# Layer 1 of an attention and two-layer MoE kernel: column tiles in pairs with banks of their own, subtractions of GpSimd tied to VectorE, wider weight pieces

## Chip, core and metric

The kernel runs on one core of one Trainium2 chip. The metric is the device time of one execution in microseconds (us). PE is TensorE, DVE is VectorE, ACT is ScalarE, POOL is GpSimd, SP is SyncE, which issues the transfers.

## What is computed

Sigmoid attention feeds a first layer with g = h cos(h), which feeds a second layer with a rational function. 4 batches of 448 tokens, 12 heads of 64 (model width 768), hidden width 2048 in both layers:

```python
attn = 1.0 / (1.0 + np.exp(-(scale * q @ k.T - np.log(S))))
x = attn @ v                                  # (1792, 768)
h = x @ w1_in;  y = (h * np.cos(h)) @ w1_out  # layer 1
h = y @ w2_in                                 # layer 2
P = a[0] + a[1]*h + a[2]*h**2 + a[3]*h**3
Q = 1.0 + abs(b[0])*abs(h) + abs(b[1])*h**2
out = (P / (Q + 1e-06)) @ w2_out
```

The four weight matrices are given as float64.

## The kernel before, in words

**Numbers.** Every operand of a product is held as a scaled pair of fp16 values (high and low part), and a product is three matmuls (high by high, high by low, low by high). No engine reads float64: a piece of weights is loaded as pairs of 32-bit words (`f64_load`, line 111), `f64_value` (line 119) puts f32 values together in three DVE passes (one tensor_scalar, two scalar_tensor_tensor, all recorded at the helpers' lines 80 and 83), a scale by row or by row of tiles comes from the largest value or from the sum of the magnitudes, and a split writes high part (ACT) and low part (DVE).

**Layer 1, per batch bt.** The 2048 hidden columns are 16 tiles f of 128. One tile is 18 matmuls of 128x448 into one PSUM bank (`h_matmul`, line 564, matmul at line 570), from a pool of four banks (`PS`, line 73; the pools stand at lines 593 and 594). A chain of operations then makes g = h cos(h): `kk` on ACT (line 854) rounds h/(2 pi) to int32 in `k`; `r0` on DVE subtracts it (`r<-hx,ck,k`); `sn` on ACT (line 861) takes the sine; `r1` on DVE multiplies by h again out of the bank (`r<-hx,kap,r`) and by that frees the bank; `gh` on ACT (line 868) writes the high half of g, `gl` on GpSimd (line 871) the low half by a subtraction. The output of layer 1 is six column blocks e of 128, each a sum over all 16 f: 48 matmuls into one bank of the same pool (`o1_unit`, line 888, matmul at line 901). For batch 0 all six e are open at once (e = 4 and 5 in one of the two-bank tiles `xv`, `yw`, made by `wide`, line 600), with f outermost; for batches 1 and 2 they come as (0,1), 2, 3, 4, 5. Batch 3's are laid between the matmuls of layer 2. All of h of a batch stands before all of its o.

**What else DVE does meanwhile.** In the stretch of layer 1 it converts w1_out (tiles `f1o`, `v1o`, `wo`; used by o of batch 0), w2_out (`f2o`, `v2o`), and w2_in, all in pieces 384 wide. w2_in is read twice: once for the largest value of a row (`w2i_max_nodes`, line 1000: a load and a TENSOR_REDUCE `m2i` for each of 36 pieces), and again for the values, which are added and subtracted among four quarters and split (`w2i_nodes`, line 1026). The split pairs go to scratch in DRAM and are streamed back in layer 2.

**What sets the order.** A planner writes one fixed order for all engines before anything runs. Each operation is a node (line 619) with an engine, an assumed duration (`C448`, `C896` and the like, lines 612 to 617), predecessors, and counted resources that it takes and gives back (`stock`, line 1542: "ps" the banks, "f64" the load slots, "g", "kr" and others). `arrange` (line 650) follows the PE order as written from line 1450 on, and for the other engines takes whichever ready node is due first. Each engine and the SP queue then run their list in order: an instruction that waits holds up those behind it on the same engine.

Of the kernel before, what the change touches and what calls it, by code (L numbers as in the profile page):

```python
# [23 lines left out]
def sigmoid_attention_moe_cos_moe_rational(  # L24
# [17 lines left out]
    P = 128  # L42
# [13 lines left out]
    up = ctx.enter_context(tc.tile_pool(name="up", bufs=34))  # L56
# [107 lines left out]
    EARLY = 0  # L164
# [49 lines left out]
    m1o, s1o, i1o = (col(n, NF) for n in ("m1o", "s1o", "i1o"))  # L214
# [12 lines left out]
    with tc.manual_schedule():  # L227
# [160 lines left out]
        def add_w1o(f):  # L388
            def fin():
                row_scale(m1o[:, f:f + 1], s1o[:, f:f + 1], i1o[:, f:f + 1], f"1o{f}")  # L390
                wo[f] = wo_tile(f, 1)

            key = ("o", f)
            cells.append(
                (
                    value_ops(st_w, key, w1_out, f, 0, DM, lambda: m1o[:, f:f + 1], f"1o_{f}"),
                    split_ops(st_w, key, lambda: wo[f], s1o[:, f:f + 1], 0, DM),
                )
            )
            after[len(cells) - 1] = ((0.6, fin), range(len(cells) - 1, len(cells)))  # L400

# [92 lines left out]
        rho, irho, kap1 = col("rho"), col("irho"), col("kap1", NF)  # L494
# [69 lines left out]
        def h_matmul(pfx, bt, f):  # L564
            ps = PS(f"h{pfx}_{bt}_{f}")
# [49 lines left out]
        class Node:  # L615

            def __init__(self, eng, dur, fn, deps=(), acq=None, rel=None, due=None, soon=False, rush=False):
                self.eng, self.dur, self.fn = eng, dur, fn
                self.deps = [d for d in deps if d is not None]
                self.acq, self.rel = acq or {}, rel or {}  # L620
                self.due, self.soon, self.rush, self.end = due, soon, rush, None
                self.users, self.weak, self.after = [], (), None
# [14 lines left out]
        def N(eng, dur, fn, deps=(), acq=None, rel=None, due=None, soon=False, rush=False):  # L637
            n = Node(eng, dur, fn, deps, acq, rel, due, soon, rush)
# [8 lines left out]
        def nop():  # L647
            pass

        def arrange(stock, groups, start):  # L650
# [53 lines left out]
            def fresh(n):  # L704
                ready[n] = max([d.end + lat(d, n) for d in n.deps], default=start)
# [29 lines left out]
            while len(queue) < total:  # L735
                best = None
                cand = []
                for n in floats:
                    t = when(n)
                    if t is not None and t <= now["PE"]:  # L740
# [28 lines left out]
                for e in ("A", "V", "G", "D"):  # L769
                    c = [(r, n) for n in avail[e] for r in (when(n),) if r is not None]  # L770
                    if not c:
# [3 lines left out]
                    b_ = (max(r, now[e]), 1, n, None)  # L775
# [8 lines left out]
                t, _, n, src = best  # L784
                if n.eng == "PE":
# [15 lines left out]
        def x_nodes():  # L801
# [6 lines left out]
            for bt in range(1, B):  # L808
                for d in range(ND):
# [16 lines left out]
        def h1_nodes(bt):  # L826
# [764 lines left out]
```

## Time and profile before

| | |
|---|---|
| Time, median of 3 runs (lowest, highest) | 1024.26 us (1024.0, 1024.3) |
| The profiled execution: its time, its span | 1022.71 us, 1020.9 us |
| Mean granted clock of TensorE in it | 0.993 |
| Instructions of DVE, ACT, POOL (whole program) | 1450, 923, 75 |
| Matmuls of h in layer 1, of o in layer 1 | 1152, 1152 |

The profile comes from one execution. Busy time counts the instructions of an engine; a window's row gives the busy time of each engine in a stretch of the span, and PEclk there is the clock that TensorE was granted, where 1.00 is the upper of its two levels, 2.4 GHz, and lower values mean that part of the stretch ran at 1.2 GHz. The waits name what ended the idle time before an instruction. The chain that ended last is followed back from the last instruction to what released each.

### The profile page before, as it was taken

The page shows a single profiled execution, that of the slowest core. Times are in us where ns is not written, and L with a number is a line of the kernel's source. Part 1 is how long each engine was busy: PE and PEld are TensorE (multiplying, and loading weights), DVE is VectorE, ACT ScalarE, POOL GpSimd, SP SyncE. Part 2 cuts the span into 40 slices and gives each one's busy share as a digit, 9 for nine tenths or more (in the row PEclk, how much of TensorE's full clock was granted, in tenths as well). Part 3 has the DMA queues.
Part 4 walks back from the last instruction along what each step waited for, and adds up shares of the span by engine and source line. Part 5 has one row for each costly group of instructions (what it writes and reads, how often), then busy time and mean ns, then how long its engine had stood idle before and what let it go on. Part 6 is the DMA issues. An engine that isn't in the chain of part 4 may idle for free.

```text
span 1020.9 us, 14605 instructions
## 1 busy us (share of the span) xinstructions
PE 994.9 (97%) x5399; PEld 501.6 (49%) x5399; DVE 805.6 (79%) x1450; ACT 600.7 (59%) x923; POOL 77.0 (8%) x75
## 2 busy tenths in 40 slices
PE   9999999889999999889999999999999999999998
PEld 4444445445555554445555455555554555555554
DVE  6999969999899899999993688889927898870000
ACT  7999967634676446644664577676506767750000
POOL 0000003310132002210032000000000000000000
PEclk9999999989999999999999999999999999999999
DMA  8788952457667885567102132133122314031320
GB/s 318 269 305 279 340 190 86 130 187 237 195 210 243 278 261 159 147 202 231 38 1 109 54 111 84 67 137 121 47 76 74 139 64 153 13 103 31 107 69 28
DMA packets 79879, 150.38 MB, mean 147 GB/s; under 512 B 6720, under 2 KB 49856, under 8 KB 77760
## 3 DMA queue, kind: packets, MB, share of 16 engines
q1 hardware_dynamic: 79520, 149.11, 44.2%
q8 instruction: 42, 0.69, 0.3%
q10 hardware_dynamic: 288, 0.34, 0.1%
q14 instruction: 29, 0.24, 0.1%
HBM read 126.62 MB, written 22.81 MB: 146 GB/s over the span
## 4 chain that ended last, share of the span: by engine, by line
PE 69%; DVE 23%; DMA 3%; ACT 2%; issue 2%; DVEq 0%; ACTq 0%
PE o L1415 21%; PE xv L1280 10%; PE o L901 9%; PE yw L1280 8%; PE v L306 7%; PE hx L570 6%; PE s L285 5%; DVE r L83 5%; DVE v2i L83 4%; DVE hl2i L83 3%; DVE v2o L83 2%; DVE v1o L83 2%; PE o_x L901 2%; DMA f2o<-in_moe_w_out_dram 2%; DVE v2i L1042 1%
## 5 line engine op out<-in xcount | busy, mean ns | idle before, releaser
L570 PE MATMUL hx<-x,wi 128*128 128x448 f16 x1152 | 219.8, 352 | 4.9 <-DVE r L83 4.9
L1415 PE MATMUL o<-g,wo 128*128 128x448 f16 x1152 | 222.2, 352 | 0.0
L901 PE MATMUL o<-g,wo 128*128 128x448 f16 x1056 | 210.6, 356 | 11.7 <-DVE r L83 11.7
L901 PEld LDWEIGHTS <-wo 128*128 128x128 f16 x1152 | 113.6, 99 | 120.1 <-issue 17.0
L570 PEld LDWEIGHTS <-wi 128*128 128x128 f16 x1152 | 112.4, 98 | 112.0 <-issue 7.9
L1415 PEld LDWEIGHTS <-wo 128*128 128x128 f16 x1152 | 112.7, 98 | 105.1
L1280 PEld LDWEIGHTS <-wi 128*128 128x128 f16 x1008 | 98.3, 98 | 98.3 <-issue 7.7
L1280 PE MATMUL xv<-ty,wi 128*128 128x448 f16 x576 | 116.8, 352 | 1.2 <-DVE t L83 1.2
L871 POOL TENSOR_TENSOR g<-r,g 128x448 f16<-128x448 f32 x64 | 76.2, 1191 | 479.1 <-ACT g L868 465.9
L1280 PE MATMUL yw<-ty,wi 128*128 128x448 f16 x432 | 89.5, 352 | 2.2 <-ACT yw L1362 1.9
L78 DVE TENSOR_SCALAR ob<-o,ig 128x448 f32<-128x448 f32 (+1 forms) x9 | 5.9, 658 | 97.4 <-PE o L1415 97.4
L83 DVE SCALAR_TENSOR_TENSOR w<-w,u 128x896 f32<-128x896 f32 x64 | 69.6, 1088 | 13.8 <-ACT u L1300 13.3
L290 ACT ACTIVATE a<-s,nlogs 128x896 f32<-128x896 f32 x72 | 69.6, 1012 | 9.2 <-PE s L285 9.0
L1443 ACT ACTIVATE ob<-o,ig 128x448 f32<-128x448 f32 x15 | 9.4, 631 | 99.0 <-PE o L1415 98.9
L306 PE MATMUL v<-a,v 128*64 128x448 f32 x288 | 63.9, 554 | 0.0
L861 ACT ACTIVATE r<-r,halfpi 128x448 f32<-128x448 f32 x64 | 42.6, 667 | 34.1 <-DVE r L83 34.0
L1300 ACT ACTIVATE t<-xv,ab,sa 128x896 f32<-128x896 f32 x16 | 17.5, 1096 | 62.1 <-PE xv L1280 62.1
L985 ACT ACTIVATE hl2i<-v2i,s2i 128x384 f16<-128x384 f32 (+1 forms) x63 | 33.0, 570 | 33.7 <-DVE v2i L1042 27.9
L868 ACT ACTIVATE g<-r 128x448 f16<-128x448 f32 x64 | 36.5, 572 | 26.4 <-DVE r L83 25.3
L83 DVE SCALAR_TENSOR_TENSOR r<-hx,ck,k 128x448 f32<-128x448 f32 x64 | 43.3, 676 | 9.1 <-ACT k L854 9.0
L1311 ACT ACTIVATE g<-t,kn 128x448 f16<-128x448 f32 x64 | 39.1, 659 | 18.2 <-DVE t L83 18.2
L854 ACT ACTIVATE k<-hx,quarter,ck 128x448 int32<-128x448 f32 x64 | 45.4, 709 | 4.8 <-PE hx L570 4.7
(168 smaller groups left out, 1321.3 us busy)
## 6 DMA issues: line engine op xcount, KB each, us to landing
wi<-wsi SPq DMA_DIRECT2D x16, 1344.0 KB, 5.8
p1o<-in_moe_w_out_dram SPq DMA_DIRECT2D x16, 768.0 KB, 5.9
f1o<-in_moe_w_out_dram SPq DMA_DIRECT2D x32, 384.0 KB, 3.6
f2o<-in_moe_w_out_dram SPq DMA_DIRECT2D x32, 384.0 KB, 3.7
f1i<-in_moe_w_in_dram SPq DMA_DIRECT2D x12, 768.0 KB, 5.8
m2i<-in_moe_w_in_dram SPq DMA_DIRECT2D x24, 384.0 KB, 4.6
f2i<-in_moe_w_in_dram SPq DMA_DIRECT2D x24, 384.0 KB, 3.7
wo<-wso SPq DMA_DIRECT2D x24, 384.0 KB, 4.4
```

Of the source, the lines that this page charges most:

```text
L83: eng.scalar_tensor_tensor(out=o, in0=i0, scalar=s, in1=i1, op0=op0, op1=op1)
L285: T.matmul(ps[:, h, :S], mqk[p, "k"][kl][r, c * P:c * P + P], mqk[p, "q"][ql][r], start=(i == 0), stop=(i == 2),)
L290: A.activation(out=t, in_=ps[:, :, :S], func=AF.Sigmoid, bias=cst["nlogs"], scale=QK)
L306: T.matmul(pvt[2 * o + j][h * D:(h + 1) * D, :S], vt[r, b * D:(b + 1) * D], at[r, h], start=c == (None if i else 0), stop=c == (NC - 1 if ...
L570: T.matmul(ps[:, :S], w[:, wl, f * P:(f + 1) * P], x[:, xl, :], start=(n == 0), stop=(n == 3 * ND - 1),)
L854: A.activation(out=st["k"], in_=st["ps"][:, :S], func=AF.Identity, scale=L1c[bt][0], bias=cst["quarter"])
L861: A.activation(out=st["r"], in_=st["r"], func=AF.Sin, scale=2.0 * math.pi, bias=cst["halfpi"])
L871: G.tensor_tensor(out=st["g"][:, 1, :], in0=st["r"], in1=st["g"][:, 0, :], op=ALU.subtract)
L901: T.matmul(acc1[bt, e][:, :S], w[:, wl, e * P:(e + 1) * P], g[:, gl, :], start=f == 0 and i == 0, stop=f == NF - 1 and i == 2,)
L1280: T.matmul(o[:, :S], w[:, d, op, wl, :], x[:, xl, :], start=start and n == 0, stop=n == 3 * NDH - 1, skip_group_check=not start,)
L1311: A.activation(out=g[:, 0, :], in_=st["t"][:, b, :], func=AF.Copy, scale=kn())
L1415: T.matmul(acc2[pr, e, b][:, :S], wo2[pr, e, f][:, wl, :], gt[2 * pr + b, f][:, gl, :], start=f == FS[0] and i == 0, stop=f == FS[-1] and ...
```

## The change

**Pairs.** The h tiles of layer 1 are made two at a time in one two-bank tile, `xv` or `yw` (resource "hp", 2), and no longer in the four "ps" banks, which stay with o. `kk`, `r0`, `sn`, `r1` and `gh` then run once for a pair, on 896 columns; only the very first pair keeps tiles of its own. For this, the scale of w1_out becomes one for a pair of row tiles (`mp1o`). `gl` stays at 448 columns.

**Order on PE.** `o1_head` makes e = 0 to 3 of a batch before the next batch's h (batch 0: f outermost over four e; batches 1 and 2: (0,1), then (2,3)). e = 4 and 5 are laid between the pairs of the next batch's h, 12 matmuls after each pair. Layer 2 keeps its order and its matmuls.

**GpSimd tied.** Where the planner can, it starts a `gl` at the time at which DVE starts an `r0` or `r1` of a pair (`cov`, `tied`): GpSimd then waits for the DVE instruction ahead of that one (`add_manual_dep`). Otherwise it places `gl` where no DVE operation marked `lk` is planned.

**Weights.** Pieces are 768 wide (w2_in also 512) in place of 384. w2_in is converted once: the f32 values are stored to DRAM (`ws_v`) and come back in 24 loads of 128x512 for the additions and the split. Its scale comes from sums of magnitudes, taken by ACT (`sum_node`), as w2_out's did, now in one sum per row tile. Three load slots in place of four; slots are cut out of two large tiles, `ua` and `ba`, by a small class (`Slots`). The planner's assumed durations change.

Cut to its core:

```diff
+            for i in range(NF // 2):
...
+                        def mm(i=i, j=j, st=st, last=i == NF // 2 - 1 and j == 1):
+                            if j == 0:
+                                st["hp"] = hp.pop(0)
+                                st["ps"] = wide(st["hp"], f"hx_{bt}_{i}")
+                            h_matmul("x", bt, 2 * i + j, st["ps"][:, j])
...
+                after(i)
...
+                    n = N("A", A896 + 2 * PTR, lambda kk=kk: kk(None), [*hn, cn, *(seam if not bt else [])], {"kr": 1}, rush=True)
+                    n = N("V", C896 + PTR, lambda r0=r0: r0(None), [n], cov=True, rush=True)
+                    n = N("A", A896 + PTR, sn, [n], rush=True)
+                    n = N("V", C896 + PTR, lambda r1=r1: r1(None), [n], rel={"hp": 1}, cov=True, rush=True)
...
+                n = N("A", A896, gh, ends, {"g": 1})
+                g0 = N("G", G448, lambda gl=gl: gl(0), [n])
...
+                before = last_of("V") if n.tied else None
                 n.fn()
+                if n.tied:
+                    tc.add_manual_dep(
+                        last_of("G"), before.name,
...
+        def sum_node(st, m, w, name, deps, due):
+            def f():
+                A.activation(out=st["junk"], in_=st["v"], func=AF.Abs, accum_out=m)
+                fs.drop(name)
...
-                    def mx(r=r, n=n, st=st):
-                        i = (r % NDH) * 2 * n_ + (r // NDH) * n_ + n
-                        f64_max(m2i[:, i:i + 1], st["f"])
...
+                    st, v3 = value_nodes(w2_in, r, c0, w, name, due, True)
+                    a_ = sum_node(st, m2i[:, i:i + 1], w, name, [v3], due)
+
+                    def out_(r=r, c0=c0, w=w, st=st, name=name):
+                        SY.dma_start(ws_v[r][:, c0:c0 + w], st["v"])
...
+                            SY.dma_start(v[x], ws_v[ids[x][0]][:, ids[x][1]:ids[x][1] + w])
...
+        def o1_head(bt):
+            for es in [range(4)] if bt == 0 else [(0, 1), (2, 3)]:
...
+        for bt in range(1, B):
+            o1_head(bt - 1)
+            tail = []
+
+            def after(i, bt=bt, tail=tail):
+                for f in (2 * i, 2 * i + 1):
+                    tail.extend(o1_unit(bt - 1, f, e, f == 0, f == NF - 1) for e in (4, 5))
...
-            "ps": 4, "u": 1, "xs": 2, "uv": 7, "f64": 4, "v": 4, "hl": 3, "kr": 5, "g": 16, "tmp": 7, "s5": 1, "wi2": 2,
+            "ps": 4, "hp": 2, "u": 1, "xs": 2, "q": 0, "qh": 0, "f64": 3, "v": 3, "hl": 3, "kr": 3, "g": 8, "g2": 0,
```

The order on DVE while PE makes h of batch 0. Before (lines 80 and 83 are the helpers; `r1` here is the tile of `r0` and `r1`, `v1o` and `wo1` are pieces of w1_out):

```order
L83 SCALAR_TENSOR_TENSOR r1_0_4_2032<-hx_0_4_1972,ck0_1786,k1_0_4_2027 128x448
L80 TENSOR_SCALAR v1o_1_0_2035<-f1o_1_0_1907 128x384
L80 TENSOR_SCALAR v1o_1_1_2038<-f1o_1_1_1914 128x384
L83 SCALAR_TENSOR_TENSOR v1o_1_0_2035<-f1o_1_0_1907,v1o_1_0_2035 128x384
L83 SCALAR_TENSOR_TENSOR r1_0_4_2032<-hx_0_4_1972,kap1_103,r1_0_4_2032 128x448
L83 SCALAR_TENSOR_TENSOR v1o_1_1_2038<-f1o_1_1_1914,v1o_1_1_2038 128x384
L83 SCALAR_TENSOR_TENSOR r1_0_5_2066<-hx_0_5_2006,ck0_1786,k1_0_5_2042 128x448
L83 SCALAR_TENSOR_TENSOR v1o_1_0_2035<-f1o_1_0_1907,v1o_1_0_2035 128x384
L83 SCALAR_TENSOR_TENSOR v1o_1_1_2038<-f1o_1_1_1914,v1o_1_1_2038 128x384
L83 SCALAR_TENSOR_TENSOR r1_0_5_2066<-hx_0_5_2006,kap1_103,r1_0_5_2066 128x448
```

With the change (`ba` holds k, r and the values, `ua` the loaded words; the helpers' lines are now 107 and 110):

```order
L110 SCALAR_TENSOR_TENSOR ba_1801<-hx_0_4_2000,ck0_1761,ba_1801 128x896
L110 SCALAR_TENSOR_TENSOR wo1_5_2075<-ba_1801,s1o_86,wo1_5_2075 128x768
L110 SCALAR_TENSOR_TENSOR ba_1801<-ua_69,ba_1801 128x768
L110 SCALAR_TENSOR_TENSOR ba_1801<-hx_0_4_2000,kap1_104,ba_1801 128x896
L107 TENSOR_SCALAR ba_1801<-ua_69 128x768
L110 SCALAR_TENSOR_TENSOR wo1_6_2104<-ba_1801,s1o_86,wo1_6_2104 128x768
L110 SCALAR_TENSOR_TENSOR ba_1801<-ua_69,ba_1801 128x768
L107 TENSOR_SCALAR ba_1801<-ba_1801 128x768
L110 SCALAR_TENSOR_TENSOR ba_1801<-hx_0_5_2055,ck0_1761,ba_1801 128x896
```

The two operations on a tile become two on a pair, and the passes between them are of 768 columns in place of 384: two between r0 and r1 of the fourth pair, four from there to the next pair.

The order on PE where the first h tile of batch 1 ends (`hx_1_0` is the tile, `o1_0_4` and `o1_0_5` are column blocks 4 and 5 of batch 0). Before:

```order
L570 MATMUL hx_1_0_3040<-x1_5_2764,wi1_5_1375 128x448
L570 LDWEIGHTS wi1_5_1375
L570 MATMUL hx_1_0_3040<-x1_5_2764,wi1_5_1375 128x448
L570 LDWEIGHTS wi1_0_295
L570 MATMUL hx_1_1_3077<-x1_0_1901,wi1_0_295 128x448
L570 LDWEIGHTS wi1_0_295
```

With the change, where the first pair of batch 1 ends:

```order
L584 MATMUL hx_1_0_2515<-ua_69,wi1_5_1360 128x448
L584 LDWEIGHTS wi1_5_1360
L584 MATMUL hx_1_0_2515<-ua_69,wi1_5_1360 128x448
L984 LDWEIGHTS wo1_0_1863
L984 MATMUL o1_0_4_2569<-ba_1801,wo1_0_1863 128x448
L984 LDWEIGHTS wo1_0_1863
L984 MATMUL o1_0_4_2569<-ba_1801,wo1_0_1863 128x448
L984 LDWEIGHTS wo1_0_1863
L984 MATMUL o1_0_4_2569<-ba_1801,wo1_0_1863 128x448
L984 LDWEIGHTS wo1_0_1863
L984 MATMUL o1_0_5_2574<-ba_1801,wo1_0_1863 128x448
L984 LDWEIGHTS wo1_0_1863
```

The next h matmul stood right behind the tile's last; now 12 matmuls of o of batch 0 stand between two pairs.

The order on DVE while PE makes h of batch 2, around the chain of a tile. Before (`v2i` values of w2_in, `f2i` its words):

```order
L83 SCALAR_TENSOR_TENSOR r1_2_5_4593<-hx_2_5_4531,ck2_3001,k1_2_5_4569 128x448
L80 TENSOR_SCALAR v2i_21_2_0_4597<-f2i_21_2_0_4434 128x384
L80 TENSOR_SCALAR v2i_22_2_0_4600<-f2i_22_2_0_4440 128x384
L83 SCALAR_TENSOR_TENSOR v2i_21_2_0_4597<-f2i_21_2_0_4434,v2i_21_2_0_4597 128x384
L83 SCALAR_TENSOR_TENSOR r1_2_5_4593<-hx_2_5_4531,kap1_103,r1_2_5_4593 128x448
L83 SCALAR_TENSOR_TENSOR v2i_22_2_0_4600<-f2i_22_2_0_4440,v2i_22_2_0_4600 128x384
L83 SCALAR_TENSOR_TENSOR v2i_21_2_0_4597<-f2i_21_2_0_4434,v2i_21_2_0_4597 128x384
L83 SCALAR_TENSOR_TENSOR v2i_22_2_0_4600<-f2i_22_2_0_4440,v2i_22_2_0_4600 128x384
L83 SCALAR_TENSOR_TENSOR r1_2_6_4633<-hx_2_6_4571,ck2_3001,k1_2_6_4627 128x448
```

With the change (128x4x128 is a split of 512 columns into `ua`, line 1168 the additions; the conversion is over here):

```order
L110 SCALAR_TENSOR_TENSOR ba_1801<-hx_2_5_3819,ck2_2673,ba_1801 128x896
L110 SCALAR_TENSOR_TENSOR ua_69<-ba_1801,s2i_1811,ua_69 128x4x128 x3
L110 SCALAR_TENSOR_TENSOR ba_1801<-hx_2_5_3819,kap1_104,ba_1801 128x896
L1168 TENSOR_TENSOR ba_1801<-ba_1801 128x512
L110 SCALAR_TENSOR_TENSOR ua_69<-ba_1801,s2i_1811,ua_69 128x4x128 x2
L1168 TENSOR_TENSOR ba_1801<-ba_1801 128x512
L110 SCALAR_TENSOR_TENSOR ua_69<-ba_1801,s2i_1811,ua_69 128x4x128 x2
L1168 TENSOR_TENSOR ba_1801<-ba_1801 128x512
L110 SCALAR_TENSOR_TENSOR ua_69<-ba_1801,s2i_1811,ua_69 128x4x128
L110 SCALAR_TENSOR_TENSOR ba_1801<-hx_2_6_3902,ck2_2673,ba_1801 128x896
```

The conversion passes of w2_in that stood between the r's are gone from this place; additions and splits of reloaded values stand there.

## Rows read from the trace of the kernel before

**Rows 1.** The page, busy time of the engines over the span
```profile
PE 994.9 (97%) x5399; PEld 501.6 (49%) x5399; DVE 805.6 (79%) x1450; ACT 600.7 (59%) x923; POOL 77.0 (8%) x75
```

**Rows 2.** The chain that ended last, in time: start, duration (us), what
```profile
141.57 3.51 PE hx L570 x18
...
493.34 54.48 PE hx L570 x288
547.82 6.81 PE o L901 x36
```

**Rows 3.** Windows: length, busy by engine (x count), PEclk, DMA share, GB/s
```profile
141.50:547.80 406.30, 389.24 (x2032) 198.97 (x2031) 379.86 (x847) 231.46 (x437) 73.07 (x61) 0.98 0.54 167
141.50:198.00 56.50, 56.50 (x301) 28.85 (x300) 48.94 (x102) 35.29 (x60) 14.35 (x12) 1.00 0.36 109
198.00:210.00 12.00, 3.95 (x14) 1.39 (x12) 12.00 (x24) 7.16 (x13) 4.38 (x4) 0.64 0.44 127
382.00:460.00 78.00, 69.48 (x353) 34.88 (x352) 78.00 (x138) 45.02 (x79) 18.69 (x16) 0.98 0.58 170
547.80:590.00 42.20, 39.95 (x212) 20.40 (x210) 21.44 (x26) 21.63 (x28) 3.10 (x3) 1.00 0.29 102
```

**Rows 4.** Waits of PE: total us, times, longest us
```profile
PE o L901 <- DVE r L83: 11.7, 5, 3.6
PE hx L570 <- DVE r L83: 4.9, 6, 1.5
```

**Rows 5.** Groups of DVE by form, 141:212; busy us, mean ns | idle before
```profile
L83 DVE SCALAR_TENSOR_TENSOR v1o<-f1o,v1o 128x384 int32<-128x384 int32 x36 | 23.6, 688 | 0.0
L83 DVE SCALAR_TENSOR_TENSOR r<-hx,ck,k 128x448 f32<-128x448 f32 x16 | 10.8, 675 | 1.2 <-ACT k L854 1.1
```

**Rows 6.** The same view of DVE, 212:395
```profile
L83 DVE SCALAR_TENSOR_TENSOR v1o<-f1o,v1o 128x384 int32<-128x384 int32 x28 | 13.7, 550 | 0.0
...
L117 DVE TENSOR_REDUCE m2i<-m2i 128x1 f32<-128x384 f32 x24 | 12.8, 544 | 2.9 <-DMA m2i<-in_moe_w_in_dram 2.9
...
L117 DVE TENSOR_REDUCE m2i<-m2i 128x1 f32<-128x256 f32 x12 | 4.8, 410 | 0.0
```

**Rows 7.** Timeline of DVE, three places: start, duration (us), instruction
```profile
60.62 0.95 DVE L83 SCALAR_TENSOR_TENSOR v1i<-f1i,v1i 128x768 int32<-128x768 int32 x1
...
62.34 0.56 DVE L80 TENSOR_SCALAR v1i<-f1i 128x768 int32<-128x768 int32 x1
62.81 1.02 DVE L83 SCALAR_TENSOR_TENSOR wi<-v1i,s1i,wi 128x768 f16<-128x768 f32 x1
63.74 0.63 DVE L262 TENSOR_TENSOR kl<-k,kh 128x448 fp32r<-128x448 f32 x1
...
301.44 0.55 DVE L83 SCALAR_TENSOR_TENSOR v2o<-f2o,v2o 128x384 int32<-128x384 int32 x1
301.91 0.68 DVE L83 SCALAR_TENSOR_TENSOR r<-hx,kap,r 128x448 f32<-128x448 f32 x1
302.50 0.80 DVE L83 SCALAR_TENSOR_TENSOR v2o<-f2o,v2o 128x384 int32<-128x384 int32 x1
...
590.34 1.15 DVE L83 SCALAR_TENSOR_TENSOR t<-t,ab,xv 128x896 f32<-128x896 f32 x1
591.40 1.15 DVE L83 SCALAR_TENSOR_TENSOR t<-yw,i_y,t 128x896 f32<-128x896 f32 x1
```

**Rows 8.** Timeline of POOL and DVE at 306 us
```profile
306.01 1.04 POOL L871 TENSOR_TENSOR g<-r,g 128x448 f16<-128x448 f32 x1 [1.70 <-ACT g L868]
306.04 1.49 DVE L83 SCALAR_TENSOR_TENSOR x<-raw,kx_x,x 128x448 f16<-128x448 f32 x1
```

**Rows 9.** Groups of ACT by form, 565:1000
```profile
L1300 ACT ACTIVATE t<-xv,ab,sa 128x896 f32<-128x896 f32 x16 | 17.5, 1096 | 62.1 <-PE xv L1280 62.1
```

**Rows 10.** The page, DMA issues: count, KB each, median us to landing
```profile
p1o<-in_moe_w_out_dram SPq DMA_DIRECT2D x16, 768.0 KB, 5.9
```

**Rows 11.** Windows, ten microseconds of the h tiles of batch 2
```profile
435.00:445.00 10.00, 8.19 (x35) 3.90 (x35) 10.00 (x20) 5.20 (x11) 1.78 (x2) 0.83 0.69 189
```

More of the change, by code (lines that the diff above doesn't have):

```diff
@@ L66, in col, with view, __init__, get @@
         return const([P, n], dt, name, tag, bufs)
+    SLOT, LENT = 4 * S, 7
+    NU = 34
+    area = {"u": up.tile([P, NU * S], I32, tag="u", name="ua", bufs=1)}
+    def view(a_, off, n, dt=F32):
+        x = area[a_][:, off // 4:off // 4 + n]
+        return x if dt == I32 else x.bitcast(dt)
+    class Slots:
+        def __init__(self, a_, offs):
+            self.free, self.kept = [(a_, o) for o in offs], {}
+        def get(self, name):
+            assert self.free, name
+            x = self.kept[name] = self.free.pop(0)
+            return x
+        def drop(self, name):
+            self.free.append(self.kept.pop(name))
+    SU = Slots("u", [i * SLOT for i in range(NU - LENT)])
+    def halves(x):
+        return x.rearrange("p (a b) -> p a b", a=2)
     def U(shape, dt, name):
-        return up.tile(shape, dt, tag="u", name=name)
+        x = view(*SU.get(name), S, dt)
+        return x if len(shape) == 2 else halves(x)
     psum = []
@@ L648, in nop, with last_of @@
             pass
+        kind = {"V": V.engine, "G": G.engine}
+        def last_of(e):
+            return next(i for i in reversed(nc.cur_bb.bb.instructions) if i.engine == kind[e])
         def arrange(stock, groups, start):
@@ L704, in fresh @@
             def fresh(n):
-                ready[n] = max([d.end + lat(d, n) for d in n.deps], default=start)
+                ready[n] = max([d.end + lat(d, n) for d in n.deps], default=start - AHEAD if n.eng == "D" else start)
                 if n.eng != "PE":
@@ L739, in arrange @@
                     t = when(n)
-                    if t is not None and t <= now["PE"]:
+                    if t is not None and (t <= now["PE"] - LATER or t <= now["PE"] and late[n] < now["PE"] + 6.0):
                         cand.append((now["PE"], 0, n, floats))
@@ L784, in arrange @@
                 t, _, n, src = best
+                if n.cov and now["G"] <= t + 0.05 and port[0] <= t + 0.05:
+                    c = [m for m in avail["G"] for r in (when(m),) if r is not None and r <= t + 0.3]
+                    if c:
+                        m = min(c, key=lambda m: late[m])
+                        m.tied = True
+                        avail["G"].remove(m)
+                        commit(m, t)
                 if n.eng == "PE":
@@ L969, in sigmoid_attention_moe_cos_moe_rational @@
         ]
[L970 removed]
+        ws_v = [drp.tile([P, DFF], F32, tag=f"wsv{r}", name=f"wsv{r}") for r in range(ND)]
+        ws_out = drp.tile([P, ND, NF, 2, P], F16, tag="wso", name="wso")
         s2i, i2i = col("s2i", NDH), col("i2i", ND)
@@ L1418, in run @@
                     )
+                if rel.get("g2"):
+                    for x in range(2):
+                        g2s.drop(f"g2_{2 * pr + x}_{f}")
             rel = dict(rel or {})
```

510 lines of the change are left out of this document (282 added, 228 removed).

## The prediction

> **What bounds the kernel now.** The page first: PE is busy 97% of the span [rows 1], so time can only come from gaps on PE, or from matmuls that ran at the lower clock. I then followed the chain that ended last in order of time. The first h matmul of layer 1 starts at 141.57 us and layer 2's first stretch (o of batch 3 beside it) at 547.82; 288 matmuls in between take 54.48 us without a gap, 0.1892 us each [rows 2]. So the stretch to which the change belongs is 406.25 us long. It holds 2016 matmuls of layer 1 (1152 of h; 3 times 288 of o), 381.4 us at that pace, and 16 others of 2032 [rows 3], products of attention and small reductions of half the work or less, for which I take 2.0 us (3.0 at the full pace). **22.9 us are lost there, and that is the most that this stretch can give.**
>
> The windows say where. From 141.5 to 198 PE is busy all of the time. From 198 to 210 it does 14 matmuls in 12 us: 12 − 14 × 0.189 = 9.4 us lost, at a granted clock of 0.64. From 382 to 460, h of batch 2, 353 matmuls stand in 78 us: 11.2 lost. Some 2.3 us lie elsewhere. In both windows DVE is busy for every microsecond [rows 3], and PE's waits there are for DVE's `r`: 11.7 us before o and 4.9 before h [rows 4]. At 198 the four banks that o needs are those of the last four h tiles, and only r1 frees a bank; DVE is behind with w1_out. So DVE's backlog is the limit there, through banks. Over the whole stretch DVE is busy 379.9 of 406.3 us, ACT only 231.5 [rows 3].
>
> **The change, part by part.** Matmuls: none added or removed, so 381.4 + 2.0 us stays.
>
> *DVE's work.* Its instructions go from 1452 to 1124. (a) The 36 maxima of w2_in go: 12.8 + 4.8 = 17.6 us [rows 6]. ACT takes 18 sums instead, about 18 × 1.0 (a pass over 896 takes 1.10 [rows 9]), and hides them, with over 170 us idle. (b) r0 and r1: 124 of 0.59 (301.91 to 302.50) become 62 of 1.06 (590.34 to 591.40) [rows 7], 73.2 − 65.7 = 7.4 us less. (c) 62 + 36 of the 328 that go are counted; 16 are small reductions for w2_out's scale, 0.15 each at most as I set them, 2.4 us; the other 214 are joins of pieces. Two passes of 384 take 2 × 0.47 (301.44 to 301.91), one of 768 takes 0.86 (two from 60.62 to 62.34) [rows 7]: 0.08 per instruction saved, and less where a 512 replaces a 384; with 0.065 that is 13.9 us. (d) Collisions: beside GpSimd's subtractions the three-operand pass of 384 took 688 ns, without them 550 [rows 5, 6]. 36 × 0.138 = 5.0 us over some 16 subtractions (12 and 4 [rows 3]), 0.31 each, so up to 64 × 0.31 = 20 us. What the tie saves of it lies between 0 and 20; r itself reads PSUM and keeps 675 ns beside the same subtractions [rows 5], so I take 15. Sum: 379.9 − 17.6 − 7.4 − 2.4 − 13.9 − 15 = 324 us in a stretch of 385, 84% in place of 93%. I do not put this in the sum: off the path it is worth nothing beyond the waits it ends.
>
> A subtraction that starts with r and ends with it leaves the next pass alone; 39 of the 64 wait for a DVE instruction in the new order, those in h of batch 0 nearly all. One placed elsewhere still blocks: at 306 us one of 1.04 starts 0.03 us before DVE's split, which takes 1.49 in place of about 0.68, 0.8 lost [rows 8]; the mean above is 0.31. The Trainium skill (SBUF — State Buffer, "Who interferes with whom") is stricter: DVE and GpSimd share one pair of ports, whichever starts first holds it for its whole instruction while the other fully blocks, and only a DVE operation with at most one SBUF input does not need it. By that rule a subtraction outside r costs up to its 1.04 us, so two uncovered ones per pair would cost 2.1, not 0.6, and r in PSUM nothing, as its 675 ns show; by the rule the tie would save more than 15 where it holds, and h of batch 0 would lose over 10 us where it does not.
>
> *Gap at 198.* o of batch 0 now needs only the four "ps" banks, which no h tile holds: nothing to wait for but g and wo. The head of four e takes 12 × 0.189 = 2.27 us per f, DVE converts one f in 0.47 + 2 × 0.86 + 0.93 = 3.12 us [rows 7]; with some nine ready at 198 the last is done near 221, while f = 15 is needed at 198 + 15 × 2.27 = 232. **9.4 us go.**
>
> *h of batch 2.* A pair with its 12 matmuls of o takes 48 × 0.189 = 9.08 us. Its bank is next wanted 12 + 48 matmuls after its end, 11.35 us. The chain that frees it: kk 1.10 [rows 9], r0 1.15, sine about 1.0, r1 1.15 [rows 7], some 0.9 for hops, 5.3 us. Slack 6 us. **11.2 us go, and the 2.3 elsewhere.**
>
> *h of batch 0* is where it is tight. No o can fill there: the bank of a pair is wanted 36 × 0.189 = 6.81 us after its end, and the chain takes 5.3. From r1 of pair 1 to r1 of pair 6 the new DVE order holds 10 r of 896, 22 passes and 7 splits of weights, 3 of x: 10.6 + 15 × 0.86 + 7 × 0.47 + 7 × 0.93 + 3 × 0.6 = 35.1 us, 7.0 per pair against 6.81. So DVE falls 0.2 us behind per pair, 1.2 over six, and each chain loses up to one pass in flight. Before, this stretch lost nothing [rows 3]. What it loses now lies between 0 and 10 us (six pairs, each r0 and r1 late by a pass of 0.86: 10.3). I take **2.0 us** new wait: 1.5 of slack less 1.2 of lag less some 0.3 of collisions per pair leaves near nothing, so only the last pairs wait.
>
> *Slots and queue.* Three slots serve the 16 pieces of w2_out and 18 of w2_in. The r0 of pair 3 of batch 2 stands behind them on DVE, and so do the scales that need ACT's sums: at 198 + 36.3 (head) + 72.6 (eight pairs) + 36.3 + 4 × 9.08 = about 380, and 6 us of slack more. From 221 that is 166 us for 34 pieces through 3 slots: 14.6 us per turn of a slot. A turn is a landing of 5.9 us [rows 10], passes of 2.2 that are spread among others to about 5, a sum of 1.0 with its wait: 12 to 13. **Nothing added.** SP's queue falls from 404 to 323 transfers; the store and the reload of f32 values replace the second reading of w2_in, and the DMA engines were used 54% [rows 3].
>
> *Layer 2* keeps its matmuls and order; the seam from 547.8 to 590 loses 42.2 − 212 × 0.189 = 2.1 us [rows 3], which I leave.
>
> **Sum.** 1022.71 (the profiled execution) − 22.9 + 2.0 = 1001.8. The median of the runs is 1.55 us above that execution: 1003.3.
>
> **Rivals.**
> 1. *h of batch 0 slips.* DVE at 7.0 us per pair against 6.81 is in lag from the start, and o has no part in that stretch. For: the ledger above. Against: 141.5 to 198 left DVE 7.6 us idle before [rows 3], and the head behind it has 11 us of margin for wo. Price: up to 10 us instead of 2, about 1011.
> 2. *More than the ceiling.* A lighter DVE reaches the seam early, and the 2.1 us there go too, with no new wait in h of batch 0: 1003.3 − 2.0 − 2.1 = about 999. Against: order and work behind the seam are the same.
> 3. *The clock takes it back*: the change doesn't bring what it says. From 435 to 445, after a wait for a bank, 35 matmuls took 10 us at 0.83 of the clock, 10 − 35 × 0.189 = 3.4 us lost [rows 11]. If every pair of h of batch 0 brought such a dip, 6 × 3.4 = 20 us, about 1021 to 1024, no change. Against: six waits of up to 1.5 us before h, 4.9 us together, stand in the stretch from 382 to 460 and its clock is 0.98 all the same [rows 3, 4]. The Trainium skill (TensorE: Matmul & The Clock Gate, "A second HAM failure mode: psum-queue depth-cycling") tells of a kernel in which small idles between groups, from banks in turn, made the clock swing between its levels; two wide banks in turn is that pattern, and by that rule this rival holds. The windows here bear it out at one place only.
> 4. *Slower: the three slots.* If a turn of a slot takes over 14.6 us, DVE waits in its list for a landing, r stands behind it, and PE behind r. Each microsecond more costs 34 / 3 = 11.3 us; 21 us of gain are used up at 16.5. At 17 it is 27 us, about 1030. For: one slot less, pieces twice as wide, the slot now kept until ACT's sum is done. Against: the terms above sum to 12 to 13.
>
> **How the numbers follow.** My forecast 0.62; rival 1 0.17; rival 2 0.10; rival 3 0.05; rival 4 0.06. The range reaches from rival 2 (999) past rival 1 (1012) and leaves out rivals 3 and 4, 0.11, and a few in a hundred at the edges. 0.2% is 2 us, about what a measurement of this kernel can tell from no change. Faster by more: cases 1, 2 and the forecast, 0.89; same 0.05; slower 0.06.
>
> **What would show it.** Right: between the first h and the end of h of batch 3 about 385.5 us; no wait of PE for `r` at the first o, nor in h of batches 1 to 3; small waits for `r` in h of batch 0; DVE some 320 to 330 us busy in layer 1; the passes beside r not longer than alone. Wrong: a clock below 0.98 in h of batch 0 (rival 3), DVE idle for DMA between 220 and 390 us (rival 4), or a stretch of layer 1 still over 395 us.

## The result, and the profile after

The change takes 999.34 us (median of four runs, 998.93 to 999.88), the kernel before 1024.13 in the same comparison; the ratio is 0.9763, with a 95% interval of 0.9746 to 0.978. The forecast was 1003.3 in a range of 999 to 1012, so the median lies 0.3 us inside the lower end. The profiled execution took 999.64 us.

The page of the kernel after, its busy time, answers to [rows 1]: 6 us less for PE, whose matmuls are the same, and 62 us less for DVE.

```profile
PE 988.8 (99%) x5399; PEld 500.6 (50%) x5399; DVE 743.8 (75%) x1122; ACT 582.2 (58%) x779; POOL 72.0 (7%) x75
```

The chain that ended last, in order of time (start, duration, what), answers to [rows 2]:

```profile
141.16 3.51 PE hx L584 x18
146.38 51.18 PE hx L584 x270
197.57 36.32 PE o L984 x192
...
522.40 9.08 PE o L984 x48
531.67 3.40 PE xv L1388 x18
```

PE now runs through layer 1 without a gap: h of batch 0 to 197.57, then the head of o at once. Of the 48 matmuls of o from 522.40 on, 12 are the last of batch 2, so the stretch that ended at 547.82 before ends here at 522.40 + 12 × 0.189 = 524.67. From the first h it is 383.51 us long, where it was 406.25: **22.74 us less**. Of the 23.07 us between the two profiled executions all but 0.33 lie there.

The windows (length, busy by engine, PEclk, DMA share, GB/s), after; they answer to [rows 3]:

```profile
141.10:524.70 383.60, 383.60 (x2033) 198.03 (x2032) 319.19 (x521) 215.09 (x297) 68.06 (x61) 1.00 0.55 174
141.10:197.60 56.50, 56.50 (x301) 28.73 (x300) 50.47 (x75) 34.16 (x40) 11.97 (x12) 1.00 0.41 140
197.60:234.00 36.40, 36.40 (x194) 18.87 (x193) 35.00 (x50) 14.27 (x20) 5.50 (x5) 1.00 0.60 197
234.00:306.60 72.60, 72.60 (x387) 37.60 (x386) 71.47 (x126) 47.65 (x72) 14.89 (x13) 1.00 0.70 229
343.00:415.60 72.60, 72.60 (x386) 37.62 (x385) 59.17 (x96) 44.92 (x64) 13.26 (x12) 1.00 0.73 224
452.00:524.70 72.70, 72.70 (x387) 37.58 (x385) 37.03 (x50) 34.53 (x43) 13.85 (x13) 1.00 0.02 5
524.70:567.00 42.30, 40.05 (x211) 20.46 (x210) 21.03 (x25) 20.01 (x25) 3.06 (x3) 1.00 0.25 95
```

PE is busy for every microsecond up to 524.70, at a granted clock of 1.00. DVE has 319 us of work in place of 380, but it is not idle evenly: 35.0 of 36.4 us in the head of batch 0 and 71.5 of 72.6 in h of batch 1, and 37 of 72.7 only in batch 3. The seam from 524.70 to 567 still loses 42.3 − 211 × 0.189 = 2.4 us.

The waits of PE in layer 1 [rows 4] have no successor: the longest two that are left lie in layer 2.

```profile
PE yw L1388 <- ACT yw L1479: 1.9, 2, 1.7
PE xv L1388 <- DVE t L110: 1.1, 2, 0.6
```

The timeline of DVE and GpSimd for pair 4 of batch 0 (start, duration, instruction) shows the tie at work:

```profile
179.10 0.67 DVE L110 SCALAR_TENSOR_TENSOR ua<-ua,kx_x 128x448 f16<-128x448 f32 x1
...
179.69 1.14 DVE L110 SCALAR_TENSOR_TENSOR ba<-hx,ck,ba 128x896 f32<-128x896 f32 x1
179.91 1.04 POOL L945 TENSOR_TENSOR ba<-ba 128x448 f16<-128x448 f32 x1 [3.76 <-ACT ua L872]
180.75 1.01 DVE L110 SCALAR_TENSOR_TENSOR wo<-ba,s1o,wo 128x768 f16<-128x768 f32 x1
...
182.56 1.14 DVE L110 SCALAR_TENSOR_TENSOR ba<-hx,kap,ba 128x896 f32<-128x896 f32 x1
...
182.71 1.04 POOL L945 TENSOR_TENSOR ba<-ba 128x448 f16<-128x448 f32 x1 [1.76 <-DVE ba L110]
183.62 0.55 DVE L107 TENSOR_SCALAR ba<-ua 128x768 int32<-128x768 int32 x1
```

The subtraction starts 0.15 to 0.22 us after `r` and ends 0.05 to 0.12 us after it; the next pass takes 1.01 or 0.55 us, as alone. From 141 to 213 us (h of batch 0 and the first part of the head) the three-operand pass of 768 takes 955 ns, where it took 950 alone [rows 7]:

```profile
L110 DVE SCALAR_TENSOR_TENSOR ba<-ua,ba 128x768 int32<-128x768 int32 x18 | 17.2, 955 | 0.0
```

Some collisions are left: over the whole of layer 1 this pass takes 980 ns.

In the timeline of pair 4 stands how close it is. Pair 4's last matmul ends at 146.38 + 162 × 0.1896 = 177.09, pair 5's at 183.92, where PE wants pair 4's bank. r1 frees it at 182.56 + 1.14 = 183.70, 0.2 us before. Over pairs 1 to 5 that margin is 0.8, 0.4, 1.0, 0.2 and 0.4 us.

### The profile page after: what moved, and what is told of

It is laid out like the page before. It is cut to its first block, busy times and chain, and to the rows that moved or that the text cites. A ratio compares the mean times of both kernels' runs of the same rounds, so it can differ in the third digit from the quotient of the medians.

```text
span 997.7 us, 13912 instructions
## 1 busy us (share of the span) xinstructions
PE 988.8 (99%) x5399; PEld 500.6 (50%) x5399; DVE 743.8 (75%) x1122; ACT 582.2 (58%) x779; POOL 72.0 (7%) x75
## 4 chain that ended last, share of the span: by engine, by line
PE 97%; ACT 1%; DVE 1%; issue 0%; DMA 0%; ACTq 0%
PE hx L584 22%; PE o L1531 21%; PE o L984 21%; PE xv L1388 10%; PE yw L1388 8%; PE v L333 7%; PE s L312 5%; PE s_None L307 1%; DVE t L110 1%; ACT u L1408 1%; DMA k<-in_k_dram 0%; ACT w L1408 0%; ACT L1408 0%; ACT yw L1479 0%; ACT a L317 0%
## 5 line engine op out<-in xcount | busy, mean ns | idle before, releaser
L984 PE MATMUL o<-ba,wo 128*128 128x448 f16 x1152 | 226.0, 352 | 0.0
L584 PE MATMUL hx<-ua,wi 128*128 128x448 f16 x1152 | 222.3, 352 | 0.0
L1531 PE MATMUL o<-ba,wo 128*128 128x448 f16 x936 | 183.2, 352 | 0.0
L1388 PE MATMUL xv<-ua,wi 128*128 128x448 f16 x576 | 116.8, 352 | 1.1 <-DVE t L110 1.1
L945 POOL TENSOR_TENSOR ba<-ba 128x448 f16<-128x448 f32 x64 | 71.1, 1114 | 458.0 <-DVE ba L107 207.6
L1388 PE MATMUL yw<-ua,wi 128*128 128x448 f16 x432 | 89.5, 352 | 2.1 <-ACT yw L1479 1.9
L110 DVE SCALAR_TENSOR_TENSOR ba<-ua,ba 128x768 int32<-128x768 int32 (+1 forms) x68 | 64.9, 954 | 0.6
L110 DVE SCALAR_TENSOR_TENSOR ba<-hx,ck,ba 128x896 f32<-128x896 f32 (+1 forms) x33 | 36.8, 1116 | 35.5 <-ACT ba L924 35.4
L924 ACT ACTIVATE ba<-hx,quarter,ck 128x896 int32<-128x896 f32 (+1 forms) x33 | 35.3, 1070 | 35.7 <-PE hx L584 35.3
L931 ACT ACTIVATE ba<-ba,halfpi 128x896 f32<-128x896 f32 x32 | 33.3, 1041 | 24.2 <-DVE ba L110 23.9
L110 DVE SCALAR_TENSOR_TENSOR ba<-hx,kap,ba 128x896 f32<-128x896 f32 (+1 forms) x33 | 36.8, 1116 | 8.6 <-ACT ba L931 8.6
```

The costliest lines, as they stand in the source:

```text
L110: eng.scalar_tensor_tensor(out=o, in0=i0, scalar=s, in1=i1, op0=op0, op1=op1)
L584: T.matmul(ps[:, :S], w[:, wl, f * P:(f + 1) * P], x[:, xl, :], start=(n == 0), stop=(n == 3 * ND - 1),)
L924: A.activation(out=o, in_=x, func=AF.Identity, scale=L1c[bt][0], bias=cst["quarter"])
L931: A.activation(out=st["r"], in_=st["r"], func=AF.Sin, scale=2.0 * math.pi, bias=cst["halfpi"])
L945: G.tensor_tensor(out=st["g"][:, j, 1, :], in0=st["r"][:, j], in1=st["g"][:, j, 0, :], op=ALU.subtract)
L984: T.matmul(acc1[bt, e][:, :S], w[:, wl, e * P:(e + 1) * P], g[:, gl, :], start=f == 0 and i == 0, stop=f == NF - 1 and i == 2,)
```

## The experiments

My theory: PE lost 22.9 us through banks that DVE freed late; the change removes that by less work on DVE and by banks of their own together, and h of batch 0 is left with a margin of 0.2 to 1.0 us, so that anything that makes DVE slower there shows at once. The rivals: the banks and the order of o alone do it, and DVE is off the path; or the lighter DVE alone does it, and the banks do not matter. Each kernel is the change with one thing altered, or with several where its section says so. All ran beside the kernel before, whose medians in the four comparisons lie between 1023.4 and 1024.1; a difference of less than about 1 us between two rows is therefore not told by the times alone.

| Kernel | Median us | Above the change (999.34) | PE's wait for r before h |
|---|---|---|---|
| untied | 1007.84 | 8.5 | 7.0 |
| passes of 384 | 1004.61 | 5.3 | 3.9 |
| sums of w2_in on DVE | 999.69 | 0.35 | none |
| all savings on DVE undone | 1029.56 | 30.2 | 25.6 |
| o not between the pairs | 1001.77 | 2.4 | 1.0 |
| h and o share banks | 1016.41 | 17.1 | none (o waits) |
| two load slots | 1011.74 | 12.4 | none (o waits) |
| all undone, planner told | 1012.67 | 13.3 | 7.1 |
| untied, planner told | 1003.64 | 4.3 | 3.1 |
| passes of 384, planner told | 1000.46 | 1.1 | 0.6 |

**Untied.**

```diff
-                if n.tied:
+                if False:
                     tc.add_manual_dep(
```

> The change without the tie: same order, but a subtraction of GpSimd starts as soon as its own operands are there. My theory: in h of batch 0 DVE frees the banks only 0.15 to 0.9 us before PE wants them, and 14 subtractions there now block DVE's weight passes, 0.3 to 0.8 us each, 0.6 to 1.6 per pair. So PE waits for r in h of batch 0, 3 to 8 us in all, and loses at most 1 us elsewhere, where a chain has 6 us of room: 1002 to 1008 us. Rival: the tie is worth nothing, since DVE is off the path: 999 to 1000, no wait for r.

Waits of PE (total us, times, longest), then the timeline of GpSimd and DVE from 164 us, then the window of layer 1, which lies from 140.50 to 532.40 here:

```profile
PE hx L584 <- DVE ba L110: 7.0, 6, 1.8
```

```profile
164.60 2.54 POOL L945 TENSOR_TENSOR ba<-ba 128x448 f16<-128x448 f32 x2 [5.39 <-ACT ba L942]
164.80 1.45 DVE L110 SCALAR_TENSOR_TENSOR ua<-ua,kx_x 128x448 f16<-128x448 f32 x1
...
166.18 1.78 DVE L110 SCALAR_TENSOR_TENSOR ba<-ua,ba 128x768 int32<-128x768 int32 x1
```

```profile
140.50:532.40 391.90, 384.89 (x2032) 197.40 (x2031) 339.57 (x521) 214.19 (x297) 87.19 (x62) 1.00 0.53 170
```

1007.84 us, at the upper end of the theory's range. Two subtractions from 164.60 to 167.14 stretch a split from 0.67 to 1.45 us and a pass from 0.95 to 1.78, 1.6 us together. DVE is busy 339.6 us in layer 1 with the same 521 records that took 319.2 in the change, 20.4 more, the upper end of the collisions in the prediction. That is what the tie takes away; the collisions that the change still has come on top. Four of the six waits, 4.3 us, lie in h of batch 0; the other two, 2.7 us, in h of batch 1, where I had allowed 1.

**Passes of 384.**

```diff
+        w = x.shape[-1]
+        if w == DM:
+            for i in range(2):
+                c = slice(i * DM // 2, (i + 1) * DM // 2)
+                f64_value(x[:, c], t[:, :, c], part)
+            return
...
+                    for c in (slice(0, DM // 2), slice(DM // 2, DM)):
+                        stt(V, wo[f][:, 1, c], st["v"][:, c], s1o[:, f // 2:f // 2 + 1], wo[f][:, 0, c], ALU.mult, ALU.subtract)
```

> The change with each 768-wide value pass and each 768-wide split of w1_out and w2_out on DVE made as two instructions of 384; loads, banks, order and tie stay. Some 0.08 us more per pass, 0.45 per pair in h of batch 0. My theory (margin there 0.15 to 0.9 us): PE waits 2 to 3 us in h of batch 0, 1001 to 1003 us. Rival (DVE off the path): 999 to 1000.

Waits of PE, and the h matmuls of the timeline of PE that waited:

```profile
PE hx L590 <- DVE ba L110: 3.9, 5, 1.6
```

```profile
170.87 13.79 PE L590 MATMUL hx<-ua,wi 128*128 128x448 f16 x72 [0.64 <-DVE ba L110]
185.68 6.98 PE L590 MATMUL hx<-ua,wi 128*128 128x448 f16 x36 [1.02 <-DVE ba L110]
192.84 6.99 PE L590 MATMUL hx<-ua,wi 128*128 128x448 f16 x36 [0.17 <-DVE ba L110]
...
282.15 6.98 PE L590 MATMUL hx<-ua,wi 128*128 128x448 f16 x36 [0.49 <-DVE ba L110]
...
293.02 6.99 PE L590 MATMUL hx<-ua,wi 128*128 128x448 f16 x36 [1.62 <-DVE ba L110]
```

1004.61 us, 1.6 more than the theory's upper end. In h of batch 0 the waits are 1.8 us, just under the 2 to 3 expected; 2.1 us more come in h of batch 1, at 282 and 293 us, which I had thought safe behind 6 us of room. DVE is full there (71.5 of 72.6 us in the change), and its passes are in a fixed order.

**Sums of w2_in on DVE.**

```diff
+                if eng == "V":
+                    V.tensor_reduce(out=m, in_=st["v"], axis=AX, op=ALU.add, apply_absolute_value=True)
```

> The change with the 18 sums of magnitudes of w2_in made by DVE (a reduction each) in place of ACT: about 12 x 0.87 + 6 x 0.6 = 14 us more on DVE, none of it in h of batch 0. My theory: DVE has some 10 us idle up to r0 of pair 3 of batch 2 and a chain there has 6 us of room, so 14 us fit: 999 to 1001 us. Rival: DVE is the limit up to there (71.5 of 72.6 us busy in h of batch 1), so most of the 14 us go onto PE: 1007 to 1013 us.

Windows of layer 1 and of h of batch 2:

```profile
141.10:524.60 383.50, 383.50 (x2030) 197.93 (x2030) 332.82 (x540) 200.84 (x261) 67.76 (x61) 1.00 0.54 174
343.00:415.60 72.60, 72.60 (x387) 37.54 (x385) 66.79 (x104) 40.25 (x53) 15.10 (x13) 1.00 0.76 233
```

999.69 us, 0.35 above the change and inside the scatter of both. DVE is 13.6 us busier in layer 1 (332.8 against 319.2), 7.6 of it in h of batch 2, where it had room; PE waits nowhere there. The theory holds. So most of what the maxima of w2_in cost (17.6 us of DVE) was worth nothing once the other savings stood.

**All savings on DVE undone.** The three edits above together, and r0 and r1 in two:

```diff
+                    for q in range(2) if j is None else ():
+                        stt(V, o[:, q], x[:, q], L1c[bt][0], k[:, q], ALU.mult, ALU.subtract)
```

> The change with its savings on DVE undone and its banks and its order of o kept: untied, passes of 384, r0 and r1 in two of 448, sums of w2_in on DVE. DVE busy some 370 to 380 us in layer 1, as before the change. My theory (DVE's backlog is what costs, the banks only give it its place): 5 to 9 us lost in h of batch 0 and 10 to 20 up to the middle of batch 2: 1015 to 1025 us. Rival: the banks and the order alone bring the gain: 1000 to 1004 us.

Waits of PE, windows, and three of the h pairs that waited:

```profile
PE hx L590 <- DVE ba L110: 25.6, 15, 3.3
```

```profile
141.10:198.00 56.90, 49.24 (x257) 24.06 (x254) 52.87 (x112) 28.82 (x33) 16.07 (x10) 1.00 0.33 114
198.00:234.00 36.00, 35.01 (x186) 17.92 (x184) 35.93 (x73) 14.64 (x17) 11.22 (x6) 1.00 0.44 152
234.00:390.00 156.00, 144.32 (x759) 73.51 (x758) 154.22 (x357) 67.39 (x94) 26.58 (x18) 1.00 0.68 221
```

```profile
295.92 6.98 PE L590 MATMUL hx<-ua,wi 128*128 128x448 f16 x36 [2.36 <-DVE ba L110]
...
383.95 6.98 PE L590 MATMUL hx<-ua,wi 128*128 128x448 f16 x36 [2.69 <-DVE ba L110]
...
499.21 8.39 PE L590 MATMUL hx<-ua,wi 128*128 128x448 f16 x36 [3.31 <-DVE ba L110]
```

1029.56 us, **slower than before the change** (ratio 1.0051, 1.0034 to 1.0067): banks of their own and the order of o bring nothing by themselves in this order, and the rival of 1000 to 1004 is out. DVE is busy 369.8 us in layer 1, 10 less than before, so not quite every saving is undone.

Fifteen pairs wait for a bank, 25.6 us. Five of these waits, 8.7 us, lie in h of batch 0, where the kernel before lost nothing up to 198 us. There a pair's bank is wanted 36 matmuls, 6.8 us, after its end; with four banks of one tile each it was wanted after three other tiles, 54 matmuls, 10.2 us. Pairs thus ask for an r that is on time. But ten waits, 16.9 us, lie in h of batches 1 to 3. There o stands between the pairs, and a bank is wanted 60 matmuls, 11.35 us, after its pair's end, which is later than before. The sooner return of the banks does not explain these; the order is the suspect, since the planner wrote it for the durations of the change. The run with a planner that is told, below, tests that.

**o not between the pairs.**

```diff
-            for es in [range(4)] if bt == 0 else [(0, 1), (2, 3)]:
+            for es in [range(4), (4, 5)] if bt == 0 else [(0, 1), (2, 3), (4, 5)]:
```

> The change with column blocks 4 and 5 of o made before the next batch's h, not between its pairs; the rest stays. A pair's bank is then wanted 6.8 us after its end in every batch, as in batch 0, in place of 11.35. My theory: DVE, nearly full in h of batch 1, frees the banks late by part of a pass: 1 to 4 us lost in batch 1, 0 to 2 in batch 2, none in batch 3: 1000 to 1005 us. Rival: without o between the pairs every chain is late: 10 us and more, from 1009 on. Second rival: the planner finds room and nothing is lost: 999 to 1000.

```profile
PE hx L584 <- DVE ba L110: 1.0, 1, 1.0
PE o L984 <- ACT ua L1007: 0.5, 1, 0.5
```

1001.77 us, as the theory had it. One pair of batch 2 waits 1.0 us and one block of o 0.5. Since the planner makes its order anew, r is on time nearly everywhere; the o between the pairs are worth about 2 us (2.4 by the medians, 1.7 by the two profiled executions).

**h and o share banks.** Blocks 0 to 3 of o take halves of the wide tiles:

```diff
+                if first and shared:
+                    if e % 2 == 0:
+                        acc1["tag", bt, e] = hp.pop(0)
+                        acc1["wide", bt, e] = wide(acc1["tag", bt, e], f"o1_{bt}_{e}")
+                    acc1[bt, e] = acc1["wide", bt, e - e % 2][:, e % 2]
```

> The change with o's blocks 0 to 3 of batches 0 to 2 in the two wide tiles of the h pairs, so that h and o share banks again; all savings on DVE stay. My theory: at the first o of batch 0 PE waits for the whole chain of the last pair, about 5 to 7 us, and nothing more elsewhere, since there other o stands between: 1004 to 1008 us. Rival: the gap of before came from DVE's backlog alone, and with a lighter DVE shared banks cost below 1 us: 999 to 1000.

Waits of PE, the first o of the timeline of PE, and the window that was lost before [rows 3]:

```profile
PE o L992 <- ACT ua L1015: 6.2, 4, 3.9
PE o L992 <- DVE ba L110: 5.9, 2, 5.3
```

```profile
198.77 1.29 PE L992 MATMUL o<-ba,wo 128*128 128x448 f16 x6 [0.61 <-DVE ba L110]
205.34 18.44 PE L992 MATMUL o<-ba,wo 128*128 128x448 f16 x87 [5.27 <-DVE ba L110]
```

```profile
198.00:210.00 12.00, 6.12 (x23) 2.51 (x23) 12.00 (x14) 6.79 (x8) 5.68 (x5) 0.72 0.56 185
```

1016.41 us, more than theory and rival had. The gap at 198 is back with a light DVE: waits of 0.61 and 5.27 us for `r`, the theory's 5 to 7, and a clock of 0.72 in the window of 12 us, 12 − 23 × 0.189 = 7.7 us lost there (9.4 before); 87 matmuls after it take 18.44 us in place of 16.46. So the shared banks are a cause of their own. The other 6.2 us of waits are those of o for ACT's copy of a neighbouring block, which this edit brought in by putting two blocks in one tile; they say nothing on the change, and the 17 us are not the price of sharing alone.

**Two load slots.**

```diff
-        fs.free.append(("b", Q0))
...
+            "ps": 4, "hp": 2, "u": 1, "xs": 2, "q": 0, "qh": 0, "f64": 2, "v": 3, "hl": 3, "kr": 3, "g": 8, "g2": 0,
```

> The change with two slots for float64 words in place of three. 166 us for 34 pieces through two slots leave 9.8 us per turn. My theory, from a landing of 4.3 us in the profile after, passes of 3 to 5 and a sum of 1 with its wait (9 to 11 us per turn): DVE waits for loads and PE loses 0 to 20 us: 999 to 1020, with DVE idle for DMA between 220 and 380 us. Rival: loads are prefetched early enough that two slots do: below 1000, DVE idle for DMA as now.

```profile
PE o L983 <- ACT wo L1062: 2.8, 3, 1.4
...
PE o L983 <- DVE wo L110: 1.9, 4, 0.5
```

```profile
198.00:244.00 46.00, 41.34 (x205) 19.69 (x203) 41.76 (x57) 20.01 (x28) 4.68 (x4) 0.96 0.44 154
```

1011.74 us, inside a wide expectation, but at another place than I had put it. PE waits for `wo` in the head of batch 0: w1_out's 16 pieces come too late through two slots, and 46 − 205 × 0.189 = 7.3 us are lost from 198 to 244. No wait of DVE for a load stands in this stretch; the planner knew of the two slots and had put DVE's passes later. Some 4 us more are lost in layer 2 after 540 us, where PE's waits for ACT and DVE come to 6.6 us in place of 3.0; why is not shown. The third slot is needed, and a rival of that kind would have struck here.

**The same with a planner that knows.** A planner that takes a pass for shorter than it is puts r behind it. So three of the edits were run again with its durations corrected (for a pass of 768 by 0.15 us in the first, as here, and by 0.08 in the others), and without tie and port rule where they are undone:

```diff
+        def pad(w):
+            return 0.15 if w == DM else 0.0
...
-            n = N("V", cost(w), p2,
+            n = N("V", cost(w) + pad(w), p2,
```

> As the run with all savings on DVE undone, but the planner is told: passes of 768 cost 0.15 us more (two instructions and collisions), r0 and r1 of a pair cost two of 448, subtractions are placed as before the change, without tie or port. It can so put w1_out's passes behind r in h of batch 0. My theory (too much work for DVE up to the middle of batch 2, whatever the order): waits move from h to o of batch 0 and to batch 2, 1010 to 1025 us. Rival: the 30 us of that run came from an order that was wrong for its costs, and banks and order of o alone bring the gain: 1000 to 1004 us.

> The change without the tie and without the planner's rule for the shared port, passes of 768 planned 0.08 us longer for the collisions. My theory: the tie is worth what DVE lacks in h of batch 0 and the planner can find a part of it elsewhere: 1001 to 1006 us, waits for r of 2 to 5 us. Rival: planning makes up for the tie: 999 to 1000 us. Second rival: it makes up for nothing, 1007 to 1008 as in the untied run.

> As the run with passes of 384, but the planner is told of 0.08 us more per pass of 768. My theory: the 5 us lost there were r late behind passes that the planner took for shorter; with w1_out's passes moved back they shrink to 0 to 2 us: 999 to 1002 us. Rival: the width itself is needed, 1004 to 1005 us as before.

The waits of PE before h for the three (all undone, untied, passes of 384), one late pair of the first, and the window of layer 1 of the second:

All undone:

```profile
PE hx L590 <- DVE ba L110: 7.1, 8, 2.0
```

```profile
195.56 8.67 PE L590 MATMUL hx<-ua,wi 128*128 128x448 f16 x36 [2.02 <-DVE ba L110]
```

Untied:

```profile
PE hx L584 <- DVE ba L110: 3.1, 2, 1.8
```

```profile
141.70:529.00 387.30, 384.19 (x2032) 197.76 (x2031) 336.37 (x522) 214.76 (x297) 86.16 (x62) 1.00 0.54 172
```

Passes of 384:

```profile
PE hx L590 <- DVE ba L110: 0.6, 1, 0.6
```

All undone but planned: 1012.67 us, so 16.9 of the 30.2 us of that run were the order. The waits in h of batches 1 to 3 fall from 16.9 to 2.8 us, and in h of batch 0 from 8.7 to 4.3. What is left there fits the banks that come round sooner, but no run shows that apart from DVE's work. Banks, order and an informed planner thus bring about 11 of the 24 to 25 us, and the savings on DVE the other 13, given these banks. The savings on DVE with the old four banks were not run; the run with shared banks comes nearest. Untied but planned: 1003.64, so tie and port rule are worth 4.3 us rather than 8.5; DVE still has 17.2 us more to do than in the change, the collisions. Passes of 384, planned: 1000.46, so the wide pieces themselves are worth about 1 us, 0.6 of it the one wait shown.

## Why the prediction was right, and where it was off

*The bound and the ceiling* were right. 22.9 us were lost between the first h and layer 2; 22.74 came back there. The gap at 198 went, h of batch 2 went, and the 2.3 us elsewhere too.

*DVE's work*: 319 us busy against 324 forecast, just below the 320 to 330 that I named as a sign. (The trace counts 1450 and 1122 instructions, not 1452 and 1124; the difference is the same.) What the tie saves is the term that I set low: 15 of up to 20 us; the untied run shows 20.4. That would account for the 5 us, if the other terms are right, which were not measured one by one. The Trainium skill's rule (SBUF — State Buffer, "Who interferes with whom") held in kind: the pass beside an untied subtraction is blocked for 0.8 us, and an r that reads PSUM is not (1.14 us beside the subtraction; an operation of its shape takes 1.15 in layer 2 [rows 7]). Its full price in h of batch 0, over 10 us, did not come: the untied run lost 4.3 there.

*h of batch 0* is the step that failed in size. I put 2.0 us of new wait there; none came. The ledger was right (DVE's r0 come 7.1 us apart, from 158.49 to 194.03 over five pairs, forecast 7.0). What I had wrong was the subtraction of lag and blocking from 1.5 us of slack: the chain of pairs 1 to 5 takes 5.8 to 6.6 us in place of 5.3 and still ends 0.2 to 1.0 us before 6.81, and the lag had built up fully only at pair 6, whose r1 ends at 196.89 + 1.14 = 198.03, 0.5 us after pair 7's last matmul, but whose bank nobody wants before the head of o is over. Rival 1 was near all the same: 0.08 us more per pass is enough to bring waits. With a margin of 0.2 us at pair 4, that none came at all is in part luck.

*The step from one execution to the median* is the other: I added the 1.55 us by which the profiled execution of before lay under its median. After the change the two differ by −0.30. Before's runs scatter over 1021.9 to 1026.3 in these comparisons, so the 1.55 us are best read as scatter and not as a term. With 2.0 and 1.85 the 4.0 us between 1003.3 and 999.34 are accounted for but for 0.1.

*Rival 2* named this number, about 999, but not its way: the seam still loses 2.4 us.

*Rival 3*, the clock: no. In the change nothing in layer 1 waits. In the run with all savings undone, two wide banks in turn with twelve waits of 0.9 to 2.7 us keep the granted clock at 1.00 up to 390 us. So the swing of the clock of which the Trainium skill tells (TensorE: Matmul & The Clock Gate, "A second HAM failure mode: psum-queue depth-cycling") did not come with these waits. It is not ruled out for all such waits: the clock falls to 0.72 behind the longer wait of the run with shared banks, and once behind waits of 2.0 us and less in the run with all undone and the planner told (last section).

*Rival 4*, the slots: 12.4 us with two of them, so too few slots do cost time, and three are enough here; the piece that is short of slots is w1_out before the head of batch 0, not w2_in before batch 2, as I had it.

*Slower than before* could have come by a way that I had not listed: an order written for shorter passes than DVE then has, together with banks that come round sooner in h of batch 0, takes 1029.56 us; the same work with the planner told takes 1012.67.

## What to carry to other kernels

A wait on a bank has three sizes: how much work stands before the instruction that frees it, how soon the bank comes round again, and what else can fill the time. Wider operations on two wide tiles in place of four narrow ones save instructions, but where nothing else fills the time a bank comes round sooner (6.8 us in place of 10.2), so they need the saved work; cost both. And a table of durations that sets a static order should be told the truth: the same instructions cost 5.3 us under a wrong one and 1.1 under a right one, and the kernel without the savings 30.2 and 13.3.

An off-path engine's work that blocks the busy one (a subtraction on GpSimd) can be put under an operation that it does not block. Here it was worth 17 to 20 us of DVE's time and 4.3 to 8.5 of the kernel's.

## What the runs showed of the hardware that I had not expected

The length of a wait alone does not tell what the clock does. Windows around two places where it fell, first in the run with all savings undone, then in the same with the planner told:

```profile
496.00:508.00 12.00, 8.79 (x39) 4.22 (x40) 12.00 (x19) 6.58 (x9) 2.73 (x2) 0.86 0.00 0
```

```profile
190.00:206.00 16.00, 13.98 (x66) 6.67 (x65) 16.00 (x29) 7.95 (x8) 5.89 (x5) 0.89 0.32 118
```

After 2.69 us of waiting at 384 us (all undone) 36 matmuls took 6.98 us, as at the upper level. After 3.31 us at 499 they took 8.39, and the granted clock was 0.86 around them. After 2.02 us at 196 (planner told) they took 8.67, at 0.89 around them. Four shorter waits, of 0.2 to 1.0 us, lie in the 31 us before that one; but in the same part of the run with all savings undone five waits of 1.0 to 2.6 us in 36 us left the matmuls at 6.98 each time. What tells these apart is not shown.
